# A fused Fourier layer and MoE layer on one core: TensorE's loop taken in pairs of steps

## The chip, the cores and the metric

The kernel runs on one core of a Trainium2 chip. The metric is the device time of one execution in microseconds, the median of several runs. The core has five engines with queues of their own: TensorE (PE, matmuls and their weight loads), VectorE (DVE), ScalarE (ACT), GpSimd (POOL) and SyncE (SP, which issues most transfers). Each works through its own queue in order and waits where an instruction needs another engine's result.

## The reference

```python
# attention part: x (8, 3008, 256), w_r, w_i (256, 256), b_r, b_i (256)
X = np.fft.rfft(x, axis=1)
Yr = Xr @ w_r - Xi @ w_i + b_r
Yi = Xr @ w_i + Xi @ w_r + b_i
Yr = np.sign(Yr) * np.maximum(np.abs(Yr) - 0.01, 0.0)      # the same for Yi
y = np.fft.irfft(Yr + 1j * Yi, n=3008, axis=1)
# second part: 24064 tokens, w_in (256, 2048), w_out (2048, 256)
h = y.reshape(24064, 256) @ w_in
g = np.where(h > 0.0, h, np.exp(np.minimum(h, 0.0)) - 1.0)
out = g @ w_out
```

## The kernel before, in words

The Fourier transform of 3008 = 47 x 64 points is done in two small transforms each way, as matmuls with tables of sines. The work on one of the 8 batches is cut into *units*, each some matmuls into one PSUM tile and a copy out of it: six A (first forward transform, L129), eight X (second, L166), twelve M (the complex weights, bias and shrinkage, L206), six B (first inverse transform, L233) and eight Y (second, L274). Between A and X and between B and Y the data goes to DRAM and back (`load_Z` L159, `load_Bs` L267), which reorders it. ACT does the copies of A, X, B and Y. In an M unit DVE adds the bias (L202) and POOL does the shrinkage (L210, L211).

The second part is cut into 376 *steps*, 47 for each batch. Step i takes one block of 512 tokens (`blk`) and two of the sixteen groups of 128 hidden columns (`fp`, eight pairs). It has three pieces:

- `front(i)`: four bfloat16 matmuls of 512 columns (L715) write `hps`, which is two PSUM banks. ACT then takes its exponential into `Et` (L729 in one piece; L724 in two halves in steps without a unit; L726 and L727, a Relu and an exponential, in steps with an M unit).
- `elu(i)` and `finish_elu()`: `elu` puts the clip of `Et` on DVE (L754) or, in steps without a unit, in halves on POOL (L752); after an M step there is none. `finish_elu`, called one step later, lets DVE combine `hps` and `Et` into `gT` (L742, or L740 after a step with an M unit or with none). This is the last reader of `hps`.
- `back(i)`: eight float32r matmuls of 256 columns (L773) add the product of `gT` and `w_out` to two PSUM tiles `ps_o`. It runs LAG = 2 steps after `front(i)`. After the eighth step of a block, DVE and ACT copy `ps_o` out (L784) and SP stores it (L791). Where `back` is called with `split`, the copy of the first tile is on DVE.

PSUM has eight banks: `psF` (one tile of two banks) holds the units' tiles, `psH` (two tiles of two banks) holds `hps`, and `psO` (two tiles of one bank) holds `ps_o`. In some of the steps without a unit (`calm`, one of three) `hps` is taken from `psF`, so that three buffers go round. `Et` and `gT` have three buffers each.

`plan(b)` puts one unit at most into each of the 47 steps of batch b (`f0`): the rest of the Y units of b itself, then X, M and B of batch b+1, the A units of b+2, and the first two Y units of b+1. In the order of the steps of batches 1 to 6 that is Y Y Y Y, X x8, M M M M B M M B Y M M B Y M M B M M B A B A A A A A Y Y and seven steps without a unit. `f1` holds loads that go with a step. The last batch has six units only.

The schedule is manual: each engine's queue holds its instructions in the order in which the program calls them. The loop at L844 therefore sets the order on all the engines: the unit of step i, `front(i)`, `finish_elu()` (which is for step i-1), the loads, `elu(i)` and `back(i-2)`, with `back` ahead of `elu` at the end of a block.

Of the kernel before, what the change touches and what calls it, by code (L numbers as in the profile page):

```python
# [29 lines left out]
def kernel(  # L30
# [14 lines left out]
    B, S, D = x.shape  # L45
# [45 lines left out]
    NPAIR = NFT // 2  # L91
    assert S * NPAIR % TB == 0 and S % (P // 2) == 0
    PER = S * NPAIR // TB
    LAG = 2
    n = B * PER
# [489 lines left out]
    def gate(src):  # L585

        t = gatep.tile([P, 1], F32, name="gate", tag="gate")
        nc.gpsimd.tensor_copy(t[0 : src.shape[0], :], src)
# [106 lines left out]
    def pieces(t, k):  # L695

        out_, c = [], 0
        while c < k:
            b, r = divmod(t + c, S)
            e = min(k, c + S - r)  # L700
            out_.append((b, r, c, e))
            c = e
        return out_

    def front(i, third, on_act, halves):
        blk, fp = divmod(i, NPAIR)
        if third:
            hps = psF.tile([P, 2, TB], F32, name="hps", tag="fps")
        else:
            hps = psH.tile([P, 2, TB], F32, name="hps", tag="hps")  # L710
        for s in range(2):
            ft = 2 * fp + s
            for b, t0, c0, c1 in sorted(pieces(blk * TB, TB), key=lambda z: z[3] - z[2]):
                for dt in range(2):
                    nc.tensor.matmul(  # L715
                        hps[:, s, c0:c1], lhsT=w_in_s[:, dt, ft * P : ft * P + P],
                        rhs=yT_of[b][:, dt, t0 : t0 + c1 - c0],
                        start=(dt == 0), stop=(dt == 1),
                    )
        Et = late3.tile([P, 2, TB], F32, name="Et", tag="Et")  # L720
        E_ = Et[:]
        if halves:
            for s in range(2):
                nc.scalar.activation(E_[:, s], hps[:, s], AF.Exp)  # L724
        elif on_act:
            nc.scalar.activation(E_, hps[:], AF.Relu, scale=-1.0)  # L726
            nc.scalar.activation(E_, E_, AF.Exp, scale=-1.0)  # L727
        else:
            nc.scalar.activation(E_, hps[:], AF.Exp)  # L729
        return hps, Et  # L730
# [15 lines left out]
    def elu(i, hps, Et, on_pool, on_act):  # L746

        E_ = Et[:]
        if on_pool:
            for s in range(2):  # L750
                eng = nc.vector if i == n - 1 and s == 0 else nc.gpsimd
                eng.tensor_scalar(E_[:, s], E_[:, s], 1.0, 0.0, ALU.min, ALU.max)  # L752
        elif not on_act:
            nc.vector.tensor_scalar(E_, E_, 1.0, -1.0, ALU.min, ALU.add)  # L754
        late_elu.append((i, hps, Et, on_pool or on_act, on_pool))

    def back(i, split):
        blk, fp = divmod(i, NPAIR)
        bs = blk * TB
        gT = g_of.pop(i)  # L760
        nq = TB // P // 2
        if fp == 0:
            po_of[blk] = [
                psO.tile([P, 2, E], F32, name="ps_o", tag="outp") for _ in range(nq)
            ]
        po = po_of[blk]
        order = [(q, s) for q in range(nq) for s in range(2)]
        if i == n - 1:
            order = [(q, s) for s in range(2) for q in range(nq)]
        for q, s in order:  # L770
            ft = 2 * fp + s
            for i_ in range(2 * q, 2 * q + 2):
                nc.tensor.matmul(  # L773
                    po[q][:, i_ % 2, :], lhsT=gT[:, s, i_ * P : i_ * P + P],
                    rhs=w_out_r[:, ft, :], start=(ft == 0 and i_ % 2 == 0),
                    stop=(ft == NFT - 1), skip_group_check=True,
                )
        if fp < NPAIR - 1:
            return
        osb = late2.tile([P, 4, E], F32, name="osb", tag="osb")  # L780
        last = i == n - 1
        for q in range(nq):
            copy = nc.vector.tensor_copy if (last and q) or (split and q == 0) else nc.scalar.copy
            copy(osb[:, 2 * q : 2 * q + 2, :], po[q][:])  # L784
            for i_ in range(2 * q, 2 * q + 2):
                for b, t, c0, c1 in pieces(bs + i_ * P, P):
                    ov = out[b * S : b * S + S, :].rearrange("(r w j) e -> w r j e", w=4, j=8)
                    while c0 < c1:
                        w, r0 = t // WT, t % WT // 8
                        k = min(c1 - c0, (w + 1) * WT - t)  # L790
                        (nc.scalar if last and i_ % 2 == 0 else nc.sync).dma_start(  # L791
                            ov[w, r0 : r0 + k // 8], osb[c0 : c0 + k, i_, :]
                        )
                        t, c0 = t + k, c0 + k
        del po_of[blk]

    def put(kind, b, *a):
        return ({"A": unit_A, "X": unit_X, "M": unit_M, "B": unit_B, "Y": unit_Y}[kind], (b, *a))

    def plan(b):  # L800

        f0 = [[] for _ in range(PER)]
        f1 = [[] for _ in range(PER)]
        n1, n2 = b + 1, b + 2
        mid = [("X", u) for u in range(8)] + [
            ("M", 0, 0), ("M", 0, 1), ("M", 1, 0), ("M", 1, 1), ("B", 0), ("M", 2, 0),
            ("M", 2, 1), ("B", 1), ("M", 3, 0), ("M", 3, 1), ("B", 2), ("M", 4, 0),
            ("M", 4, 1), ("B", 3), ("M", 5, 0), ("M", 5, 1), ("B", 4),
            ("A", 0), ("B", 5), ("A", 1), ("A", 2), ("A", 3), ("A", 4),
        ]  # L810
        if n1 < B:
            lead, seq = int(b == 0), [("y", u) for u in range(2, 6)] + mid
            seq.insert(20 if b else 4, ("y", 6))
            seq.insert(24 if b else 5, ("y", 7))
            xs = (3, 8, 13)
            seq += [("A", 5), ("n", 0), ("n", 1)] if b else [("n", 0), ("n", 1), ("A", 5)]
        else:
            lead, seq = 0, [("y", u) for u in range(2, 8)]
        for t, u in enumerate(seq, lead):
            if u[0] == "y":  # L820
                f0[t].append(put("Y", b, u[1]))
            elif u[0] == "n":
                f0[t].append(put("Y", n1, u[1]))
            elif u[0] == "A":
                if n2 < B:
                    f0[t].append(put("A", n2, u[1]))
            else:
                f0[t].append(put(u[0], n1, *u[1:]))
            if u == ("A", 1):
                f1[t] += [(load_Bs, (n1, w)) for w in range(4)]  # L830
            if u == ("A", 5) and n2 < B:
                f1[t] += [(load_Z, (n2, s0, s1)) for s0, s1 in ((0, 8), (8, NS))]
        if b == 0:
            f1[3].append((scale_w_in, (3, True, 0)))
            f1[4].append((scale_w_in, (3, True, 1)))
            f1[xs[0]].append((lambda: gate(Z_of[1][:, 16, 0:1]), ()))
        if n2 < B:
            for ci in range(3):
                f1[xs[ci]].append((load_x, (n2, ci)))
        return f0, f1  # L840

    f0 = f1 = None
    bare = 0
    for i in range(n + LAG):  # L844
        if i < n:
            r = i % PER
            if r == 0:
                f0, f1 = plan(i // PER)
                used = [bool(u0 or u1) for u0, u1 in zip(f0, f1)]
            free = not used[r]  # L850
            bare = bare + 1 if free else 0
            calm = free and (i >= n - 2 or (r + 2 < PER and not used[r + 1] and not used[r + 2]))
            for f, a in f0[r]:
                f(*a)
            on_act = any(f is unit_M for f, a in f0[r])
            h = front(i, calm and bare % 3 == 1, on_act, free and i > 0)
        finish_elu()
        if i < n:
            for f, a in f1[r]:
                f(*a)  # L860
            split = i > LAG and (i - LAG) % NPAIR == NPAIR - 1
            if split:
                back(i - LAG, True)
            elu(i, *h, free and i > 0, on_act)
        else:
            split = False
        if i >= LAG and not split:
            back(i - LAG, False)


# [28 lines left out]
```

## Time and profile before

| | |
|---|---|
| median of three runs | 911.94 us (911.36 to 913.53) |
| the profiled execution | 911.36 us, span 909.6 us, granted clock 0.997 |
| TensorE busy | 893.2 us, 6721 matmuls |
| DVE, ACT, POOL busy | 717.5, 696.8, 314.9 us |
| first layers (L715) | 1728 matmuls |
| second layers (L773) | 3008 matmuls, 301 ns each as shown |

A matmul's shown duration runs from its start to the modelled end of its result, so consecutive ones overlap and their durations can't be added; what a group costs is the distance between starts, or its piece in the chain of work. In a row of the timeline "x4" is four instructions in a row that were merged. A wait in square brackets is the idle time of that engine just before, and who ended it.

### The profile page before, as it was taken

How to read it: one execution, taken by the hardware profiler on the slowest of the kernel's cores; microseconds unless marked ns; L12 is line 12 of the kernel's file. 1: busy time of each engine (PE TensorE's matmuls, PEld its weight loads, DVE VectorE, ACT ScalarE, POOL GpSimd, SP SyncE). 2: the span in 40 equal slices, each digit the busy share in tenths (PEclk: the TensorE clock that was granted, in tenths of full speed). 3: DMA queues.
4: the chain of work that ended last, by engine and by line, in shares of the span. 5: the costliest groups of instructions: out<-in, count | busy, mean ns of one | idle time of the engine just before them, and what ended most of it. 6: DMA issues, size and time to landing. Idle time of an engine off the chain costs nothing.

```text
span 909.6 us, 17270 instructions
## 1 busy us (share of the span) xinstructions
PE 893.2 (98%) x6721; PEld 652.3 (72%) x6721; DVE 717.5 (79%) x891; ACT 696.8 (77%) x850; POOL 314.9 (35%) x438
## 2 busy tenths in 40 slices
PE   8989999999999999999999999999999999999997
PEld 3447667876688667886678766787667866777775
DVE  8669778887788778897788877888778877778776
ACT  6768788777878778787787888778887877767664
POOL 6701540333321441405404153033332134443664
PEclk9999999999999999999999999999999999999999
DMA  8997116721283215732166032752228111231011
GB/s 270 309 269 228 47 48 186 209 70 47 77 241 124 71 47 143 190 109 85 56 201 194 24 99 59 217 161 72 69 72 230 30 42 47 82 82 48 24 48 46
DMA packets 90670, 106.24 MB, mean 117 GB/s; under 512 B 5270, under 2 KB 81308, under 8 KB 87228
## 3 DMA queue, kind: packets, MB, share of 16 engines
q1 hardware_dynamic: 84332, 77.62, 30.6%
q0 software_dynamic: 5968, 27.26, 9.1%
q8 instruction: 52, 0.85, 0.4%
q10 hardware_dynamic: 288, 0.26, 0.1%
q14 instruction: 30, 0.25, 0.1%
HBM read 55.32 MB, written 49.81 MB: 116 GB/s over the span
## 4 chain that ended last, share of the span: by engine, by line
PE 85%; DVE 5%; ACT 3%; DMA 3%; issue 2%; POOL 1%; SPq 1%; DVEq 0%; ACTq 0%; POOLq 0%
PE ps_o L773 34%; PE hps L715 34%; PE mps L192 9%; PE yps L282 2%; PE bps L244 2%; PE xps L175 2%; PE aps L144 2%; DMA Bs<-DB 2%; DVE gT L742 1%; DVE Et L754 1%; ACT Et L729 1%; ACT Et L726 1%; DMA xt<-in_x_dram 1%; DVE osb L784 1%; ACT Bz L257 1%
## 5 line engine op out<-in xcount | busy, mean ns | idle before, releaser
L773 PE MATMUL ps_o<-w_out_r,gT 128*128 128x256 f32 x3008 | 477.0, 301 | 0.2 <-DVE gT L740 0.2
L773 PEld LDWEIGHTS ps_o<-w_out_r,gT 128*128 128x128 f32 x3008 | 403.4, 189 | 50.3 <-DVE osb L784 1.3
L715 PE MATMUL hps<-yT,w_in_s 128*128 128x512 bf16 (+4 forms) x1728 | 389.9, 353 | 2.5 <-DVE gT L742 1.2
L740 DVE SCALAR_TENSOR_TENSOR gT<-Et,hps 128x512 fp32r<-128x512 f32 (+1 forms) x272 | 222.8, 848 | 75.3 <-POOL Et L752 38.2
L742 DVE SCALAR_TENSOR_TENSOR gT<-hps,Et 128x1024 fp32r<-128x1024 f32 x198 | 242.2, 1223 | 16.5 <-PE ps_o L773 1.0
L715 PEld LDWEIGHTS <-w_in_s 128*128 128x128 bf16 x1728 | 141.6, 98 | 129.4 <-issue 23.0
L729 ACT ACTIVATE Et<-hps 128x1024 f32<-128x1024 f32 x198 | 204.0, 1030 | 13.2 <-PE hps L715 6.7
L752 POOL TENSOR_SCALAR Et<-Et 128x512 f32<-128x512 f32 x187 | 111.4, 615 | 222.9 <-ACT Et L724 222.9
L754 DVE TENSOR_SCALAR Et<-Et 128x1024 f32<-128x1024 f32 x198 | 137.0, 692 | 48.0 <-ACT Et L729 40.1
L210 POOL TENSOR_SCALAR clip<-yb 128x512 f32<-128x512 f32 x84 | 51.7, 615 | 316.0 <-DVE yb L202 278.6
L724 ACT ACTIVATE Et<-hps 128x512 f32<-128x512 f32 x188 | 102.1, 595 | 63.9 <-PE hps L715 63.9
L726 ACT ACTIVATE Et<-hps 128x1024 f32<-128x1024 f32 x84 | 86.3, 1027 | 71.5 <-PE hps L715 71.0
L211 POOL TENSOR_TENSOR Y<-yb,clip 128x512 bf16<-128x512 f32 x84 | 107.2, 1276 | 7.0
L727 ACT ACTIVATE Et<-Et 128x1024 f32<-128x1024 f32 x84 | 88.8, 1058 | 2.7
L202 DVE TENSOR_TENSOR yb<-mps,bias_bc 128x512 f32<-128x512 f32 x89 | 61.4, 689 | 35.4 <-PE mps L192 28.6
L127 ACT CAST XT<-xps 128x768 bf16<-128x768 f32 x61 | 48.8, 800 | 15.8 <-PE xps L175 15.8
L127 ACT CAST yT<-yps 128x752 bf16<-128x752 f32 x63 | 49.7, 788 | 14.2 <-PE yps L282 14.1
L192 PE MATMUL mps<-wcat_r,XT 128*128 128x512 bf16 x192 | 58.2, 384 | 0.8 <-ACT Bz L257 0.3
L127 ACT CAST A<-aps 128x1024 bf16<-128x1024 f32 x45 | 45.6, 1014 | 15.3 <-PE aps L144 13.8
L192 PE MATMUL mps<-wcat_s,XT 128*128 128x512 bf16 x192 | 57.1, 379 | 0.0
L192 PEld LDWEIGHTS <-XT 128*128 128x128 bf16 x384 | 30.8, 98 | 29.6 <-DVE XT L125 0.6
L257 ACT CAST Bz<-bps 128x1024 bf16<-128x1024 f32 x46 | 46.0, 1000 | 2.5 <-PE bps L244 2.5
(110 smaller groups left out, 412.9 us busy)
## 6 DMA issues: line engine op xcount, KB each, us to landing
xt<-in_x_dram POOLq DMA_DIRECT2D x21, 1024.0 KB, 7.1
out_dram<-osb SPq DMA_DIRECT2D x158, 128.0 KB
Bs<-DB SPq DMA_DIRECT2D x32, 384.0 KB
DA<-A SPq DMA_DIRECT2D x21, 512.0 KB
DB<-Bz SPq DMA_DIRECT2D x21, 512.0 KB
Z<-DA SPq DMA_DIRECT2D x7, 1152.0 KB
Z<-DA SPq DMA_DIRECT2D x11, 384.0 KB
xt<-in_x_dram POOLq DMA_DIRECT2D x6, 512.0 KB, 5.9
```

The lines of the kernel that those rows point to most:

```text
L127: nc.scalar.copy(dst, src)
L192: nc.tensor.matmul(ps, lhsT=XT[:, dt, c, o : o + P], rhs=wm[:, dt, :], start=(not biased and m == 0 and dt == 0), stop=(m == 1 and dt == 1),)
L211: nc.gpsimd.tensor_tensor(Y_of[b, q][:, i, :], yb, clip[:], ALU.subtract)
L715: nc.tensor.matmul(hps[:, s, c0:c1], lhsT=w_in_s[:, dt, ft * P : ft * P + P], rhs=yT_of[b][:, dt, t0 : t0 + c1 - c0], start=(dt == 0), sto ...
L724: nc.scalar.activation(E_[:, s], hps[:, s], AF.Exp)
L726: nc.scalar.activation(E_, hps[:], AF.Relu, scale=-1.0)
L729: nc.scalar.activation(E_, hps[:], AF.Exp)
L740: nc.vector.scalar_tensor_tensor(o, e, -1.0, h, ALU.add, ALU.max)
L742: nc.vector.scalar_tensor_tensor(o, h, 0.0, e, ALU.max, ALU.add)
L752: eng.tensor_scalar(E_[:, s], E_[:, s], 1.0, 0.0, ALU.min, ALU.max)
L754: nc.vector.tensor_scalar(E_, E_, 1.0, -1.0, ALU.min, ALU.add)
L773: nc.tensor.matmul(po[q][:, i_ % 2, :], lhsT=gT[:, s, i_ * P : i_ * P + P], rhs=w_out_r[:, ft, :], start=(ft == 0 and i_ % 2 == 0), stop=( ...
```

## The change

The loop takes two steps at a time. TensorE's order in a pair of steps i (even) and i+1 becomes: the unit of i, `front(i)`, `front(i+1)`, the unit of i+1, `back(i-2)`, `back(i-1)`. `begin` holds what was the first half of a step; with `unit_first` false it calls `front` ahead of the unit. DVE's order in a pair becomes: what the unit of i has on DVE, `finish_elu` for step i-1, the clip of i, what the unit of i+1 has on DVE, `finish_elu` for i, and the clip of i+1. At the end of a block both `back` are called ahead of the second `elu`. The plans of all batches are made first, and `calm` looks across the end of a batch. After the loop come the last `finish_elu` and the last two `back`. The units, the steps, the tiles and the buffers stay as they are.

```diff
-    f0 = f1 = None
-    bare = 0
-    for i in range(n + LAG):
-        if i < n:
-            r = i % PER
-            if r == 0:
-                f0, f1 = plan(i // PER)
-                used = [bool(u0 or u1) for u0, u1 in zip(f0, f1)]
-            free = not used[r]
-            bare = bare + 1 if free else 0
-            calm = free and (i >= n - 2 or (r + 2 < PER and not used[r + 1] and not used[r + 2]))
-            for f, a in f0[r]:
+    plans = [plan(b) for b in range(B)]
+    state = {"bare": 0}
+
+    def at(i):
+        b, r = divmod(i, PER)
+        return plans[b][0][r], plans[b][1][r]
+
+    def free_at(i):
+        return i < n and not any(at(i))
+
+    def begin(i, unit_first):
+
+        f0, f1 = at(i)
+        free = free_at(i)
+        state["bare"] = state["bare"] + 1 if free else 0
+        calm = free and (i >= n - 2 or (free_at(i + 1) and free_at(i + 2)))
+        on_act = any(f is unit_M for f, a in f0)
+        if unit_first:
+            for f, a in f0:
                 f(*a)
-            on_act = any(f is unit_M for f, a in f0[r])
-            h = front(i, calm and bare % 3 == 1, on_act, free and i > 0)
+        h = front(i, calm and state["bare"] % 3 == 1, on_act, free and i > 0)
+        if not unit_first:
+            for f, a in f0:
+                f(*a)
         finish_elu()
-        if i < n:
-            for f, a in f1[r]:
-                f(*a)
-            split = i > LAG and (i - LAG) % NPAIR == NPAIR - 1
-            if split:
-                back(i - LAG, True)
-            elu(i, *h, free and i > 0, on_act)
-        else:
-            split = False
+        for f, a in f1:
+            f(*a)
+        return (i, *h, free and i > 0, on_act)
+
+    for i in range(0, n, 2):
+        elu(*begin(i, True))
+        e = begin(i + 1, False)
+        split = i + 1 > LAG and (i + 1 - LAG) % NPAIR == NPAIR - 1
+        if split:
+            back(i - LAG, False)
+            back(i + 1 - LAG, True)
+        elu(*e)
         if i >= LAG and not split:
             back(i - LAG, False)
+            back(i + 1 - LAG, False)
+    finish_elu()
+    back(n - 2, False)
+    back(n - 1, False)
```

## The prediction

> **What bounds the kernel now.** I read the page's busy shares first, then TensorE's own waits, then the chain of work in one stretch, then the order of instructions in two kinds of step.
>
> ```profile
> PE 893.2 (98%) x6721; PEld 652.3 (72%) x6721; DVE 717.5 (79%) x891; ACT 696.8 (77%) x850; POOL 314.9 (35%) x438
> ```
> TensorE's waits (who waited for whom; total us, times, longest us):
> ```profile
> PE yps L282 <- DMA Bs<-DB: 2.9, 3, 1.0
> PE hps L715 <- DVE gT L742: 1.2, 2, 1.0
> ```
>
> TensorE is busy for 98% of the span and its longest visible waits add up to a few microseconds: its own stream of matmuls is the bound. The chain of work gives that stream's pieces (start, us, what).
>
> ```profile
> 405.08 0.36 PE xps L175 x8
> 405.43 0.87 PE hps L715 x4
> 406.30 0.92 PE ps_o L773 x8
> ...
> 862.41 0.88 PE hps L715 x4
> 863.29 0.92 PE ps_o L773 x8
> ...
> 204.33 0.97 PE hps L715 x4
> 205.30 0.92 PE ps_o L773 x8
> 206.22 0.88 PE mps L192 x4
> ```
>
> I call a step's unit U, its first layer F (hps), its second layer B (ps_o). F lasts 0.86, B 0.92, an X or Y unit 0.36, an M unit 0.88. Now the timeline (start, us, engine, line) of a stretch of X steps, and of one of M steps:
>
> ```profile
> 400.98 1.03 PE L715 MATMUL hps<-yT,w_in_s 128*128 128x512 bf16 x4
> 402.04 1.03 ACT L729 ACTIVATE Et<-hps 128x1024 f32<-128x1024 f32 x1
> 403.10 0.69 DVE L754 TENSOR_SCALAR Et<-Et 128x1024 f32<-128x1024 f32 x1
> 403.12 1.03 PE L715 MATMUL hps<-yT,w_in_s 128*128 128x512 bf16 x4
> 403.90 1.23 DVE L742 SCALAR_TENSOR_TENSOR gT<-hps,Et 128x1024 fp32r<-128x1024 f32 x1
> ...
> 405.27 1.03 PE L715 MATMUL hps<-yT,w_in_s 128*128 128x512 bf16 x4
> ```
> ```profile
> 414.89 1.06 ACT L727 ACTIVATE Et<-Et 128x1024 f32<-128x1024 f32 x1
> 415.00 0.59 PE L192 MATMUL mps<-wcat_s,XT 128*128 128x512 bf16 x2
> 415.43 1.03 PE L715 MATMUL hps<-yT,w_in_s 128*128 128x512 bf16 x4
> 415.63 0.69 DVE L202 TENSOR_TENSOR yb<-mps,bias_bc 128x512 f32<-128x512 f32 x1 [0.84 <-PE mps L192]
> 416.24 1.21 DVE L740 SCALAR_TENSOR_TENSOR gT<-Et,hps 128x1024 fp32r<-128x1024 f32 x1
> ...
> 418.12 1.03 PE L715 MATMUL hps<-yT,w_in_s 128*128 128x512 bf16 x4
> ```
>
> What to see: an F may start only when its PSUM buffer hps is free, and psH has two. So F of step i+2 waits for the DVE instruction that reads hps of step i; I call it G (L740 or L742). In the X stretch G of the step whose F began at 400.98 ends at 403.90 + 1.23 = 405.13, and F two steps on starts at 405.27: the reserve is about 0.1 us. In the M stretch G(i-1) ends at 417.45 and F(i+1) starts at 418.12: reserve 0.7. TensorE is the bound, but the ring of hps, ScalarE's exponential and DVE is almost as long.
>
> **The change part by part.** All in the profiled execution: 911.36 us, span 909.6 and 1.8 around it; 0.06% under the median of 911.94. The loop has 376 steps, 188 pairs. TensorE's order goes from U F B U F B to U F F U B B; nothing is computed more or less.
>
> *Fewer switches between bfloat16 and float32.* F after a B lasts 0.88, F after a unit 0.86; second-layer matmuls in the run follow each other by 0.113, so eight are 0.907 where the group shows 0.92. A return trip is thus 0.03, and one per pair goes: 188 x 0.03 = -5.6 us. Bounds: 0 (the unit between the Fs may take the price) and -11 (0.06).
>
> *The second F stands right behind the first.* In before, B(i-2) and U(i+1) lie between F(i) and F(i+1) and cover G(i-1). Now F(i+1) would start 0.86 after F(i). Put into the M rows: at 415.43 + 0.86 = 416.29, but G(i-1) ends at 417.45, and a first layer that waited for a G started 0.06 behind it (G from 781.76 for 1.22, F at 783.04): 417.51, so 1.22 late. Behind the waiting F on TensorE stand U(i+1) and both Bs, so nothing fills the hole. In the X rows it is 405.19 against 403.98: 1.21. Whether that lasts depends on what else moves.
>
> *M units in the first place of a pair.* DVE works in order, and the bias addition of U(i) (L202) is issued ahead of G(i-1). It ends 0.04 + 0.69 after U(i)'s last matmul, while F(i) runs; G(i-1) follows, with 1.21. This holds however long the pair gets, since G(i-1) is tied to U(i) of the same pair: 1.22 each time. By the plan (12 M units in each of 7 batches, 47 steps a batch, so pairs fall differently in odd and even batches) 6 of a batch's M units are first in a pair: 42 pairs x 1.22 = 51 us.
>
> *Pairs without an M in first place.* From F(i)'s last matmul, 0: exponential to 1.06, L754 1.09 to 1.78, G(i) 1.89 to 3.12; then, DVE's next instruction starting 0.08 before the end of an unrelated one (416.24 against 415.63 + 0.69), L754 of i+1 3.04 to 3.73, G(i+1) 3.84 to 5.07. F(i+3) then has its last matmul at 5.07 + 0.06 + 1.02 = 6.15. A pair of X lasts 2 x 2.14 - 0.03 = 4.25, so without a wait it would be at 4.25 + 0.86 = 5.11: a wait of about 1.03. That makes the pair 5.28, DVE catches up, and the next pair waits for nothing; then again. Mean 0.51. Of such pairs behind another such pair (X, Y, A and mixed) I count 71: 36 us. A pair with its M or B in second place and an M pair before it comes out at no wait (6.2 us of TensorE against G at 5.97). Bounds for the 71: 0.3 each if DVE overlaps more, 1.03 if the alternation fails: 21 to 73.
>
> *Steps without a unit* (94, 41 of them in the last batch) take their clip on POOL and halves, and a third buffer (psF) in one of three steps, so a buffer returns three first layers later: with exponentials 1.09, POOL 1.19 and G halves 1.29 from the rows at 850 to 860, G(i+1) ends 3.95 after F(i), in time. Only at the end of a run, where the third buffer is not taken, it is 3.95 + 0.06 + 1.02 - 3.57 - 0.86 = 0.6 late, 7 times: 4 us.
>
> *The output copy.* Every fourth pair writes a block: DVE's copy (L784, 0.68) stands ahead of the second L754 and waits for both Bs, at 0.86 + 0.36 + 1.84 = 3.06. It pushes L754 of i+1 from 3.04 to 3.67, 0.63 later; in a pair that already waited 1.03, 1.7 later, for which the following pair waits less. There are 46 in the loop. By walking them through the plan: 18 in X, Y or A pairs at 0.7, 5 after M M at 0.67, 3 after M B at 1.6, 3 at 0.33, the rest (free steps, or an M pair next) 0: 22 us; bounds 10 and 35. In before the same copy lies under B.
>
> *What else moves.* Units in second place follow F(i+1), and ScalarE then takes the exponential of i+1 before their copies; psF is free again 0.3 us before the next unit, which costs nothing while TensorE waits anyway. Their stores on SP and the Bs and Z loads behind them go out up to one F (0.86) later, and the two stores of a block together; five steps lie between the Bs loads and the unit that reads them, and they get longer, so 0, with 3 either way (the waits for Bs above are 2.9). x loads on POOL sit behind the same clip as before: 0. The 1.3 us that weight loads wait for L784 goes.
>
> Sum: 911.36 - 5.6 + 51 + 36 + 4 + 22 = 1019.
>
> *The clock.* The granted clock is 0.997 over the whole, and the waits of about 1 us that before has do not lower it, so the sum holds none. The Trainium skill (TensorE: Matmul & The Clock Gate, A second HAM failure mode: psum-queue depth-cycling) says that TensorE cycling through PSUM buffers with short idle spells between groups made the clock swing between half and full rate; no trace here shows it. By the row the sum stays 1019; by that rule it is the fourth rival below.
>
> **The rivals.**
> Only M pairs wait: if in the others L754 and G run closer than I have them, 911.4 - 5.6 + 51 = 957. For it: DVE is 79% busy. Against: the reserve of 0.1 in the X rows, where a whole B and U still lie between.
> Every pair waits in full: the 1.2 read from the X rows stays in all 71: 911.4 - 5.6 + 51 + 85 + 4 + 30 = 1076. Against: DVE has less than 4.1 us of work in a pair of 5.5.
> Faster: the saved switches are all that shows, 911.4 - 5.6 = 906. It needs G(i-1) to end before F(i) does, at every pair; the point is F(i)'s start + 0.8, and the rows put it at + 2.0 in both stretches. Only a dependency on hps other than two buffers in turn could do it.
> The clock falls: if it halves wherever TensorE stalls by 1.2 us, the 42 M pairs (5.3 us of matmul each) take 224 us more, 1243.
>
> **How the numbers follow.** Forecast 0.66, only M pairs 0.13, every pair 0.13, faster 0.04, clock 0.03, no change 0.01. The forecast's own range, with its bounds, is 980 to 1050; to leave out no more than 2 in 10 the range takes in the first rival and most of the second: 955 to 1062. About 0.3% is what a measurement tells from no change: faster 0.04, same 0.01, slower 0.95.
>
> **What would show it.** TensorE waiting for DVE gT (L740, L742), at L715, about 110 us in total, longest near 1.7; over 1 us at each pair that begins with an M unit, just behind its first F; about every second X pair; hardly any in the last 70 us; granted clock still near 1.00. In the last stretch a pair of 3.57 for 3.60. The forecast is wrong if F(i+1) starts 0.86 behind F(i) in X and M steps, or if another engine's wait takes the place of this one.

## The result and the profile after

| | before | the pairs |
|---|---|---|
| median | 912.66 us | 1012.92 us (1010.2 to 1013.47, 6 runs) |
| ratio | | 1.1096, 95% interval 1.1081 to 1.1110 |
| profiled execution: time, span | 911.36, 909.6 us | 1012.27, 1010.5 us |
| granted clock | 0.997 | 0.996 |
| TensorE busy share | 98% | 90% |

The pairs cost 100 us. First the busy shares on the page of the changed kernel:

```profile
PE 911.4 (90%) x6721; PEld 636.9 (63%) x6721; DVE 711.9 (70%) x891; ACT 691.3 (68%) x850; POOL 313.4 (31%) x438
```

All engines have the same instructions and nearly the same busy time; what grew is TensorE's idle time. Who it waits for, in the view of waits of TensorE (total us, times, longest us):

```profile
PE hps L715 <- DVE gT L742: 50.8, 55, 2.1
PE hps L715 <- DVE gT L740: 33.1, 39, 1.1
PE yps L282 <- ACT yT L127: 1.5, 1, 1.5
```

Before, the same view had 1.2 us in two waits for gT. Now there are 94 waits with 83.9 us. A wait costs more than its shown idle time: without one, a matmul starts 0.16 before the shown end of the one ahead, and that overlap is lost too, which makes 83.9 + 94 x 0.16 = 99 us.

Next the timeline of a pair of two M steps (start, us, engine, line; F, B and U are again a first layer, a second layer and a unit, G is DVE's L740 or L742):

```profile
343.38 1.03 PE L715 MATMUL hps<-yT,w_in_s 128*128 128x512 bf16 x4
...
343.58 0.69 DVE L202 TENSOR_TENSOR yb<-mps,bias_bc 128x512 f32<-128x512 f32 x1 [0.95 <-PE mps L192]
344.19 1.21 DVE L740 SCALAR_TENSOR_TENSOR gT<-Et,hps 128x1024 fp32r<-128x1024 f32 x1
...
345.45 1.04 PE L715 MATMUL hps<-yT,w_in_s 128*128 128x512 bf16 x4 [1.05 <-DVE gT L740]
...
347.00 2.23 PE L773 MATMUL ps_o<-w_out_r,gT 128*128 128x256 f32 x16
```

The second F starts 2.07 behind the first, not 0.86: it starts 0.05 behind the end of G(i-1), which stood behind the bias addition of this pair's own unit. Two X pairs follow each other like this:

```profile
322.12 1.89 PE L715 MATMUL hps<-yT,w_in_s 128*128 128x512 bf16 x8
...
325.05 1.22 DVE L742 SCALAR_TENSOR_TENSOR gT<-hps,Et 128x1024 fp32r<-128x1024 f32 x1
326.09 0.52 PE L175 MATMUL xps<-M,Z 96*128 96x96 bf16 x8
326.19 0.68 DVE L754 TENSOR_SCALAR Et<-Et 128x1024 f32<-128x1024 f32 x1
326.40 0.79 PEld L715 LDWEIGHTS <-w_in_s 128*128 128x128 bf16 x5
326.44 1.03 PE L715 MATMUL hps<-yT,w_in_s 128*128 128x512 bf16 x4
...
326.97 1.23 DVE L742 SCALAR_TENSOR_TENSOR gT<-hps,Et 128x1024 fp32r<-128x1024 f32 x1
...
328.25 1.02 PE L715 MATMUL hps<-yT,w_in_s 128*128 128x512 bf16 x4 [0.78 <-DVE gT L742]
```

In the first pair the two Fs are one run of eight, with no wait; in the next the second F waits for a G that ends at 328.20. The pair after has none again. That is the alternation.

By the starts and ends of the matmuls in the whole trace (idle time before an F plus 0.163), the 42 pairs that begin with an M unit wait 1.21 to 1.42 each, 53.5 us together; the others 51 us, with 12 of the 24 X X pairs waiting and 0.52 on average over them. By the same count before has 1.8 and 8.2 us, so the change added 51.7 and 43.2.

### The profile page after: what moved, and what is told of

Its sections match the earlier page's. It is cut to its first block, busy times and chain, and to the rows that moved or that the text cites. A ratio compares the mean times of both kernels' runs of the same rounds, so it can differ in the third digit from the quotient of the medians.

```text
span 1010.5 us, 17269 instructions
## 1 busy us (share of the span) xinstructions
PE 911.4 (90%) x6721; PEld 636.9 (63%) x6721; DVE 711.9 (70%) x891; ACT 691.3 (68%) x850; POOL 313.4 (31%) x438
## 5 line engine op out<-in xcount | busy, mean ns | idle before, releaser
L715 PE MATMUL hps<-yT,w_in_s 128*128 128x512 bf16 (+4 forms) x1728 | 375.8, 353 | 85.2 <-DVE gT L742 50.8
L773 PE MATMUL ps_o<-w_out_r,gT 128*128 128x256 f32 x3008 | 405.3, 288 | 0.3 <-DVE gT L740 0.3
L773 PEld LDWEIGHTS ps_o<-w_out_r,gT 128*128 128x128 f32 x3008 | 372.1, 189 | 18.7 <-issue 4.6
L715 PEld LDWEIGHTS <-w_in_s 128*128 128x128 bf16 x1728 | 147.7, 98 | 252.1 <-issue 83.7
L740 DVE SCALAR_TENSOR_TENSOR gT<-Et,hps 128x512 fp32r<-128x512 f32 (+1 forms) x272 | 218.9, 845 | 64.7 <-POOL Et L752 44.3
L742 DVE SCALAR_TENSOR_TENSOR gT<-hps,Et 128x1024 fp32r<-128x1024 f32 x198 | 242.1, 1222 | 18.1 <-DMA DA<-A 2.6
L729 ACT ACTIVATE Et<-hps 128x1024 f32<-128x1024 f32 x198 | 199.5, 1026 | 36.6 <-PE hps L715 29.8
L726 ACT ACTIVATE Et<-hps 128x1024 f32<-128x1024 f32 x84 | 86.0, 1024 | 92.3 <-PE hps L715 91.9
L724 ACT ACTIVATE Et<-hps 128x512 f32<-128x512 f32 x188 | 98.2, 603 | 60.0 <-PE hps L715 59.9
L192 PEld LDWEIGHTS <-XT 128*128 128x128 bf16 x384 | 34.1, 98 | 37.3 <-DVE XT L125 0.6
```

What stands on the lines that cost most here:

```text
L192: nc.tensor.matmul(ps, lhsT=XT[:, dt, c, o : o + P], rhs=wm[:, dt, :], start=(not biased and m == 0 and dt == 0), stop=(m == 1 and dt == 1),)
L715: nc.tensor.matmul(hps[:, s, c0:c1], lhsT=w_in_s[:, dt, ft * P : ft * P + P], rhs=yT_of[b][:, dt, t0 : t0 + c1 - c0], start=(dt == 0), sto ...
L740: nc.vector.scalar_tensor_tensor(o, e, -1.0, h, ALU.add, ALU.max)
L742: nc.vector.scalar_tensor_tensor(o, h, 0.0, e, ALU.max, ALU.add)
L773: nc.tensor.matmul(po[q][:, i_ % 2, :], lhsT=gT[:, s, i_ * P : i_ * P + P], rhs=w_out_r[:, ft, :], start=(ft == 0 and i_ % 2 == 0), stop=( ...
```

## The experiments

The theory: F(i+1) waits for G(i-1), which frees its buffer; how late G is follows from DVE's order. The rivals: the place of the units, and DVE's or ScalarE's total work; that TensorE's order itself costs something was left to be measured.

### G ahead of the first unit

```diff
         if unit_first:
+            finish_elu()
             for f, a in f0:
                 f(*a)
```


> The pairs as changed, but DVE's combination of step i-1 (G, the last reader of hps) is issued ahead of the unit in first place, so that it no longer stands behind the bias addition L202. TensorE's order is the same. If the waits of the pairs that begin with an M unit come from DVE's order (42 of them at 1.28 us in the changed kernel's trace), they fall to 0.3 to 0.6 each and the time goes from 1013 to 970 to 985. If they come from TensorE's order alone, units behind the second first layer, the time stays at 1013.

Measured: 979.32 us, 1.0734 (1.0703 to 1.0766) of before, 34 less than the pairs. The waits of TensorE in this kernel, same columns as above:

```profile
PE hps L715 <- DVE gT L742: 33.5, 43, 3.3
PE hps L715 <- DVE gT L740: 7.7, 23, 0.9
PE mps L192 <- ACT Bz L257: 3.8, 8, 0.6
PE yps L282 <- ACT Bz L257: 3.1, 6, 0.6
```

TensorE's order is the same, so it was DVE's order that held the M pairs: their waits at F fall from 53.5 to 5.0 us. The time falls by less, because others grow by 5 us and the last two lines are new, with a third for A units (2.0 us): the unit after a B unit now waits for psF. These waits come back below.

### The second clip ahead of the copy, and no copy on DVE

The first edit issues `elu` of the second step ahead of both `back` also at the end of a block:

```diff
-        if split:
-            back(i - LAG, False)
-            back(i + 1 - LAG, True)
         elu(*e)
-        if i >= LAG and not split:
+        if i >= LAG:
             back(i - LAG, False)
-            back(i + 1 - LAG, False)
+            back(i + 1 - LAG, split)
```


> The pairs as changed, but at the end of a block the second clip (L754) is issued ahead of both second layers and the output copy, so DVE's copy no longer holds it up. The copy still stands ahead of the next G. If the copy's place costs what the prediction said (22 us for 46 copies), about a third to a half comes back: 1001 to 1008. If the copy hides in pairs that wait anyway, 1013.

Measured: 1008.33 us, ratio 1.1053 (1.1020 to 1.1085): 4.6 less than the pairs, a little less than was expected.

The second has the same order and passes `False` for `split`, so both copies of a block are ScalarE's.

> The pairs as changed, with both output copies of a block on ScalarE behind the second clip, so that DVE has none in the loop. If the copies cost the 22 us of the prediction, 990 to 995. By e2_copy_last, which brought back 4.6 us, the copy's own 0.68 on DVE is what may be left: 1000 to 1006. ScalarE may be late with the next exponential instead; then no gain.

Measured: 1001.57 us, ratio 1.0976 (1.0954 to 1.0998), 11 less than the pairs. These 11 are net of what ScalarE then loses, but the waits say nearly the same. Counted as above, though only where the trace names G as the releaser, the pairs that begin with an M unit wait 53.5 us with and without the copies, and the others 46 with them and 34 without. So the copies cost some 12 us, and not the 22 of the prediction's sum.

### The unit between the two first layers

```diff
-        e = begin(i + 1, False)
+        e = begin(i + 1, True)
```


> The second unit goes back between the two first layers: unit, first layer, unit, first layer, two second layers. If the wait is for hps and G, the unit covers 0.88 of 1.28 in M pairs and 0.36 of 1.03 in X and Y pairs: 42 x 0.9 and 71 x 0.18 less, 955 to 970. If the place of the unit behind the second first layer were itself the cause (its copy late, psF late), about 912.

Measured: 967.67 us, ratio 1.0607 (1.0576 to 1.0638), inside the expectation of the theory and far from 912. Waits of TensorE:

```profile
PE hps L715 <- DVE gT L740: 11.9, 24, 0.9
PE hps L715 <- DVE gT L742: 7.2, 13, 2.6
PE aps L144 <- ACT A L127: 2.8, 12, 0.3
PE xps L175 <- ACT XT L127: 1.6, 6, 0.7
```

The waits for G shrink by what the unit covers, and short waits of a unit for psF appear, since two units are now only one F apart.

### The three edits together

> The three edits before this together: unit, first layer, unit, first layer, two second layers; G ahead of both units; the second clip ahead of the copy. By the ring of hps the M pairs wait for next to nothing, X, Y and A pairs 0.33 on average, the copies some 8 us: 925 to 945. If pairs could be had without waits for hps, below 912.

Measured: 979.77 us, ratio 1.0739 (1.0708 to 1.0771): missed, and slower than the unit between alone. Waits of TensorE:

```profile
PE mps L192 <- DVE yb L202: 18.3, 24, 1.6
PE bps L244 <- DVE yb L202: 7.8, 18, 0.5
PE hps L715 <- DVE gT L742: 6.5, 12, 2.7
```

G ahead of the unit makes the bias addition late, and that is the reader that frees psF for the next unit, now one F away. The wait went from one ring of PSUM to the other. I had counted only hps.

### Less work on DVE in X, Y and A steps

On top of `e1_g_first`, `begin` returns `soft` in place of `free and i > 0`:

```diff
-        h = front(i, calm and state["bare"] % 3 == 1, on_act, free and i > 0)
+        soft = i > 0 and not any(f is unit_M or f is unit_B for f, a in f0)
+        h = front(i, calm and state["bare"] % 3 == 1, on_act, soft)
...
-        return (i, *h, free and i > 0, on_act)
+        return (i, *h, soft, on_act)
```


> As e1_g_first, and in the steps with an X, Y or A unit the clip moves from DVE to POOL in halves, as it is in steps without a unit. DVE then has 1.29 a step there for 1.92, and G(i+1) ends about 3.95 after F(i) for 5.07. If the waits of X, Y and A pairs come from DVE's chain of clip, G, clip, G, they go (some 37 us of 979): 940 to 950. If they come from the place of the second first layer alone, whatever DVE does, 979.

Measured: 962.90 us, ratio 1.0552 (1.0531 to 1.0573), between the two. TensorE waits 2.25 us at the first layer of step 3 and 6.15 at that of step 5. The second wait comes from the edit: the clip of step 3 now stands on POOL behind a gate (L588) that waits for the load of Z. The first does not: the clip of step 1 is done by 62.66, and G then waits on DVE for the store of an A tile that lies in one of gT's buffers. The changed kernel has that wait too, with 2.05. POOL's, DVE's and TensorE's timelines there, and busy times by windows (PE, PEld, DVE, ACT, POOL, then granted clock, DMA share, GB/s):

```profile
76.03 0.18 POOL L588 CAST gate<-Z 96x1 f32<-96x1 bf16 x1 [10.49 <-DMA Z<-DA]
...
77.15 2.37 POOL L752 TENSOR_SCALAR Et<-Et 128x512 f32<-128x512 f32 x4
```
```profile
64.49 1.28 DVE L740 SCALAR_TENSOR_TENSOR gT<-Et,hps 128x512 fp32r<-128x512 f32 x2 [2.71 <-DMA DA<-A]
```
```profile
65.83 1.86 PE L715 MATMUL hps<-yT,w_in_s 128*128 128x512 bf16 x4 [2.25 <-DVE gT L740]
...
79.18 1.86 PE L715 MATMUL hps<-yT,w_in_s 128*128 128x512 bf16 x4 [6.15 <-DVE gT L740]
```
```profile
50.00:58.00 8.00, 6.20 (x38) 2.76 (x37) 4.61 (x5) 3.76 (x4) 0.00 (x0) 1.00 0.78 230
58.00:66.00 8.00, 4.46 (x26) 2.28 (x26) 3.26 (x5) 4.66 (x7) 4.04 (x6) 0.71 1.16 325
66.00:74.00 8.00, 7.03 (x40) 5.27 (x39) 1.57 (x3) 3.48 (x6) 0.00 (x0) 0.65 1.11 257
74.00:82.00 8.00, 2.82 (x14) 1.71 (x14) 3.16 (x5) 1.07 (x3) 3.40 (x7) 0.56 0.42 136
82.00:90.00 8.00, 7.95 (x64) 6.83 (x64) 3.41 (x6) 4.38 (x8) 3.72 (x7) 0.80 0.00 0
90.00:98.00 8.00, 7.65 (x66) 5.69 (x66) 4.84 (x9) 7.34 (x13) 4.43 (x9) 1.00 0.64 195
```

So this run mixes two things, and the next one takes the gate out of the way by leaving the clip of steps 1 to 8 on DVE: `soft` is also false there unless the step is free.

> As e7_clip_on_pool, but steps 1 to 8 with a Y or X unit keep the clip on DVE, so that no clip stands on POOL behind the gate that waits for a load there (in e7_clip_on_pool TensorE waited 2.2 and 6.2 us in these steps, and the granted clock fell to 0.56 to 0.80 between 58 and 90 us). Step 8 began 9.4 us later there than in the changed kernel: 953. If the fall of the clock was not due to that gate, it is there again, and 963.

Measured: 955.14 us, ratio 1.0472 (1.0442 to 1.0502). The time is close to the 953 that was expected. The clock's part is not clean: it still falls once at the start, to 0.60 between 66 and 74 us, for a shorter time. The wait for the store is still there, with 3.73 us at the first layer of step 3. Against `e1_g_first` DVE's shorter chain brings 24 us, of some 37 that the X, Y and A pairs waited.

Then both output copies go to ScalarE here too:

> As e11_clip_on_pool_later, and both output copies on ScalarE behind the second clip, as in e8_copies_on_act. If the terms are separate, the 11 us of e8_copies_on_act come back here too: 942, and what stays over 912 is the order's own price of 15 and some leftover waits. If the copies cost only where DVE was the chain that set the pair, 950 to 955.

Measured: 946.24 us, ratio 1.0374 (1.0344 to 1.0405), between the two expectations: the copies give another 9. Waits of TensorE:

```profile
PE hps L715 <- DVE gT L740: 7.2, 24, 0.4
PE hps L715 <- DVE gT L742: 3.7, 2, 2.9
PE yps L282 <- ACT Bz L257: 3.5, 6, 0.6
PE mps L192 <- ACT Bz L257: 3.4, 8, 0.6
PE aps L144 <- ACT Bz L257: 2.3, 4, 0.6
```

With most waits for G gone, 34 us over before are left. In the count by matmul starts and ends 25 us are still idle time in front of an F, where before has 10. Next to it stand the units' waits for ScalarE, which the hps ring had hidden.

### The price of TensorE's order alone

Two pairs of kernels take G's wait on hps away, one of each pair with the loop of before, one with the pairs. The first lets G read Et twice:

```diff
-                o, h, e = gT[:, s], hps[:, s], Et[:, s]
+                o, h, e = gT[:, s], Et[:, s], Et[:, s]
```


> The pairs as changed, but DVE's combination reads Et twice and hps not at all, so hps is free as soon as ScalarE has read it; the output is then not the reference's (the positive part of the activation is left out). DVE has as many instructions as before. If the 100 us are waits for hps, nearly all of them go: 905 to 920. If DVE or ScalarE is the bound of the pairs, the time stays above 980.

> The same edit in the kernel before (the positive part of the activation is left out). It has about 10 us of waits at first layers, most of them not for hps: 905 to 912. The difference between the pairs and the single steps, both without the wait for hps, is the price of TensorE's order itself: the prediction has 5.6 us less for the pairs, the rows of the changed kernel's last stretch (3.63 a pair against 3.60 for two steps) some 5 us more.

Measured: 943.76 us for the pairs, ratio 1.0354 (1.0332 to 1.0376), and 934.29 for the single steps, 1.0243 (1.0227 to 1.0258). Both are above what was expected, so the edit does more than it was meant to: reading two operands from SBUF, G slows POOL and is slowed (see the last section). What it does show is that of the 100 us between pairs and steps only 9.5 are left when hps is free early. It also speaks against DVE's total work as the cause: DVE is busy for 825.4 us in these pairs and for 711.9 in the changed kernel, and yet they are 69 us faster.

The second makes G one instruction with one source:

```diff
-                if whole:
-                    nc.vector.scalar_tensor_tensor(o, e, -1.0, h, ALU.add, ALU.max)
-                else:
-                    nc.vector.scalar_tensor_tensor(o, h, 0.0, e, ALU.max, ALU.add)
+                nc.vector.tensor_scalar(o, e, -1.0, 0.0, ALU.add, ALU.max)
```


> The pairs as changed, with G as one instruction with Et as its only source (the part of the activation that reads hps is left out, so the output is not the reference's). hps is free after ScalarE has read it, and DVE is well below TensorE's time. What is left against the same edit in single steps is the price of TensorE's order itself: 5.6 less by the prediction; by the ends of matmuls in the traces about 3 more (a float32r group behind an X or Y unit 0.08 later, behind a B unit 0.23 later, against 0.01 saved at each switch that goes).

> The same edit in the kernel before (the part of the activation that reads hps is left out). POOL should be as fast as in before, unlike in e5_ring_off_steps, since DVE has no two-source reads of SBUF: 903 to 912. Where DVE's one-source form slows POOL too, 920 to 935.

Measured: pairs 923.48 us, ratio 1.0121 (1.0106 to 1.0136); steps 908.15, 0.9948 (0.9931 to 0.9965). The order costs 15.3 us where the prediction had a gain of 5.6 and I now had 3. Waits of TensorE in the pairs:

```profile
PE mps L192 <- ACT Bz L257: 4.7, 8, 0.6
PE yps L282 <- ACT Bz L257: 3.5, 6, 0.6
PE aps L144 <- ACT Bz L257: 2.3, 4, 0.6
```

These 18 waits of 10.5 us, with another 3.3 in front of weight loads of A units, are units that wait for psF after a B unit in second place: ScalarE copies it (1.0 us) only after the exponential of the second step. In the changed kernel a waiting F covers them. The rest is in the chain of work of the same kernel (start, us, what; L770 is the L773 of the others):

```profile
402.30 1.89 PE ps_o L770 x16
...
415.78 1.83 PE ps_o L770 x16
...
385.34 1.88 PE ps_o L770 x16
```

Sixteen second-layer matmuls cost 1.89 behind an X unit and 1.83 behind an M unit; the first of them ends 0.19 behind the last matmul of an X or Y unit and 0.31 behind that of a B unit, against 0.12 behind an F or an M unit. In a run without units (the 1.88) there is no unit to blame: there all sixteen follow each other by 0.118, where in the last stretch of before the last five of each eight follow by 0.113. Why a long run keeps the slower pace stays open.

## Why the prediction was right

The forecast of 1019 stands against 1012.9 measured, inside both ranges.

*The second F right behind the first.* Right, and shown: with hps free early 85 to 91 of the 100 us between pairs and steps go, with the G of M pairs issued earlier 34.

*M units in first place.* 42 x 1.22 = 51 against 51.7 that the change added in 42 pairs; the reading of the M rows carried over almost unchanged, as it should, since G(i-1) and the waiting F hang on the same unit.

*Pairs without an M in first place.* Right in kind, too large in size. X X pairs wait in 12 cases of 24, with 0.94 in most of those that do not follow a copy. Their mean of 0.52 is close to the predicted 0.51 only by chance, since it has the copies in it and the 0.51 did not; without copies on DVE (`e8_copies_on_act`) it is 0.40. With the end of the free runs and the copies I had 62; the change added 43.

*The output copy.* Here is the larger part of that: 22 in the sum, some 12 by the waits. In the changed kernel the X X pairs right behind a copy wait 1.13 to 1.47, which is 0.2 to 0.5 more than 0.94 and not the 0.7 of the sum.

*Fewer switches.* Wrong in sign. The step that failed is "a return trip is thus 0.03, and one per pair goes": it priced the switch where a first layer stands next to a second one, and took it for nothing where a small unit now stands there. Behind an X, Y or B unit the first float32r matmul ends 0.07 to 0.20 later than behind an F. A likely reason, not tested, is its weight load: it takes 0.19 as shown, against 0.10 for bfloat16, and the short last matmul of such a unit covers little of it. The saving fails without any unit as well: in the last stretch a pair lasts 3.63, not the 3.57 that I named, for the slower pace of the sixteen:

```profile
955.50 1.90 PE L715 MATMUL hps<-yT,w_in_s 128*128 128x512 bf16 x8
...
959.13 0.61 PE L715 MATMUL hps<-yT,w_in_s 128*128 128x512 bf16 x2
```

*What else moves.* "psF is free again 0.3 us before the next unit, which costs nothing while TensorE waits anyway" held in the changed kernel, but for B units the reserve was not there at all; with the cover gone it is worth about 12 us.

*The clock.* The forecast held: 0.996, and 1.00 between 300 and 400 us, with waits of 1.2 in the M pairs. Its ground was weaker than I wrote, for in before too the clock is at 0.50 between 58 and 60 us, behind waits of 1.01 and 0.54 close together. The rule of the Trainium skill (TensorE: Matmul & The Clock Gate, A second HAM failure mode: psum-queue depth-cycling), by which such a rhythm of short idle spells makes the clock swing, did not show in that stretch. A second fall did show at the start, where several waits come close together: 0.79 between 66 and 74 us, where before has 1.00.

That the sum came so close is partly luck. Of the 100.9 us between the two profiled executions, 95 are idle time in front of first layers, where the sum had 113: 19 too much for pairs without an M in first place and their copies. The other 6 are nearly all a slower pace of the matmuls, the lower clock at the start included, where the sum had a gain of 5.6. The two misses nearly cancel.

Of the rivals, "only M pairs" (957) falls with the 51 us elsewhere; "every pair in full" (1076) with the alternation; "faster" with every F in the rows above. None of these versions with pairs beats the loop of before: even without any wait for hps they are 15 us behind single steps with the same edit.

## What to carry to other kernels

Before putting two like pieces of work next to each other, find the last reader of the first one's buffer and lay its end beside the new start: the distance in the old trace (2.0 us from F to the end of G) against the new one (0.86) gave the loss of the M pairs almost to the number. Look in the same way at every ring the moved work touches; a wait removed from one PSUM ring came back on the other. A price read at one boundary (a large bfloat16 group against float32r) does not hold at another (a group of small matmuls).

## What the runs showed that I had not expected

POOL slows down when DVE reads two operands from SBUF. In `e5_ring_off_steps`, where G reads Et twice, the shrinkage's clip takes 1522 ns on POOL; with G reading hps from PSUM, in the changed kernel, it takes 613. First the changed kernel's groups by line, then those of `e5_ring_off_steps` (busy us, mean ns, idle before):

```profile
L740 DVE SCALAR_TENSOR_TENSOR gT<-Et,hps 128x512 fp32r<-128x512 f32 x188 | 118.0, 681 | 44.5 <-POOL Et L752 44.3
L210 POOL TENSOR_SCALAR clip<-yb 128x512 f32<-128x512 f32 x84 | 51.5, 613 | 397.9 <-DVE yb L202 351.8 <-PE hps L715 46.1
```
```profile
L740 DVE SCALAR_TENSOR_TENSOR gT<-Et 128x512 fp32r<-128x512 f32 x188 | 180.2, 1023 | 8.2 <-POOL Et L752 5.6 <-PE hps L715 2.5
L210 POOL TENSOR_SCALAR clip<-yb 128x512 f32<-128x512 f32 x84 | 127.8, 1522 | 226.8 <-DVE yb L202 223.4 <-PE ps_o L773 3.2
```

Both sides lose: G's halves go from 681 to 1023 ns. The Trainium skill says the same (SBUF — State Buffer, SBUF: two separate sides): DVE and GpSimd share a pair of ports, and a DVE instruction with two SBUF inputs and a GpSimd one that reads SBUF lock each other out. So the operand in PSUM is also what keeps POOL fast here. With one source in SBUF (`e10_one_source_steps`) the same clip still takes 962 ns on POOL, against my expectation that it would be as fast as in before. The 22 us that the single steps lose in `e5_ring_off_steps` are not lost there; but G is also shorter in that kernel, so these runs do not say how much of the 22 us is POOL's.

The clock falls around a few long waits and comes back: in `e7_clip_on_pool`, with waits of 2.25 and 6.15 us, it was at 0.56 in the window of the second and back at 1.00 some 10 us after it, while waits of 1.2 us in every M pair of the changed kernel left it at 1.00 between 300 and 400 us.
